# Wave 0's loads in another order: pairs of heads two at a time first, single pairs last, with fewer filling products

## The chip, the cores and the metric

The kernel runs on one core of a Trainium2 chip. Its time is the device time of one execution in microseconds; where a kernel was run several times, the median is given. The engines are named as in the profile: PE (TensorE), PEld (its weight loads), DVE (VectorE), ACT (ScalarE), POOL (GpSimd), SP (SyncE, which here issues nearly all transfers). A transfer moves data between HBM and the on-chip memory (SBUF) and is carried out by 16 DMA engines.

## The reference

Two stages. The first is a decaying linear attention over q, k, v of shape (4 batches, 8 heads, 768 positions, 64), in blocks of positions; `lam` is the decay of each head. The second is a feed-forward layer with a quick gelu on the attention's output, 3072 tokens of 512 features, 2048 hidden ones.

```python
for b in range(nb):                      # blocks of 64 positions
    intra = np.einsum('bhic,bhjc->bhij', qb, kb) * Dmask[None]
    intra = np.einsum('bhij,bhjd->bhid', intra, vb)
    inter = np.einsum('bhid,bhde->bhie', qb * lam_pow[None], kv_state)
    out[:, :, sl] = intra + inter
    kv_state = lam_block[None, :, None, None] * kv_state \
        + np.einsum('bhsd,bhse->bhde', kb * rev_pow[None], vb)
...
h = x @ w_in
g = h * (1.0 / (1.0 + np.exp(-1.702 * h)))
return g @ w_out
```

## The kernel before, in words

The work goes in six waves of 512 tokens. A wave first does its attention, which leaves `xT` (features by tokens, one part per pair of heads), then the first product with w_in (`mlp1`, L511) with the gelu on ACT (L517), then the second product with w_out (`mlp2`, L539). Attention of a later wave is spread among the feed-forward products of the wave before it. Wave 0 has nothing to hide behind: at the start the chip has no data, and everything has to be loaded.

Waves 0 and 1 are special. They take 256 positions of two batches each, so that wave 0 covers batches 0 and 1, and their unit of work is one batch and one pair of heads: (bl, p), bl 0 or 1, p 0 to 3. `UNITS` (L167 to L171) is the order of wave 0's eight units, and the same loop queues their loads: for each entry (bl, p, n) one transfer each for k, q and v, holding n pairs of heads, 128 KB per pair (`load_units`, L86). All are issued by SP except the very first q, which ACT issues (L89).

All loads land in a ring of 50 half slots of 128 KB (`ring`, L83). The function `pump` (L128) hands out places in the order in which the loads were queued: wave 0's q, k, v, then 16 pieces of w_in (256 KB each), seven of the eight halves of w_out (512 KB each), then the loads of wave 1 with the eighth half of w_out among them, then wave 2. A load of more than one half slot starts at an even place. A place is taken again when the load before it there has been read.

For each unit the steps are, in the order of the loop L575 to L610: cast k times its decay (`u_cast_kq` with i=0, on DVE, L280) and q (i=1, on POOL, L280), both one unit ahead; cast v (POOL, L288); turn both by four transposing products (`u_turn`, PE, L298) and copy them from PSUM (L306 on ACT, L308 on DVE); in the next round the scores (L320), the state's product kv (L345), the masking (DVE, L325) and the state's copy (L353 on ACT, L355 on DVE); in the round after that the two output products (L385, L394) and the copy to `xT` (ACT, L398). Before each `u_turn` stands `fill(FILL[i])` (L592): that many 128-column fp32 products of zeros (L271), four to an instruction, which the profile shows as two matmuls for each instruction. `fill(FILL0)` (L568) does 12 of them at the very start. They compute nothing that is used.

Weights are cast to bf16 from the ring piece by piece (`cast_w`, L157): rows 0 to 2 of w_in on POOL (L585, L590), behind the last units' casts in its queue, the others on DVE as they come (L611). Three slices of the first product are begun early: contraction part kc needs the pair kc of both batches and row kc of w_in (L597, L609, L615). The second product of wave 0 runs over the four quarters of w_out in turn (L702), so that it uses w_out as it arrives.

Every engine works through its own queue in order, except that PE takes weight loads ahead.

Of the kernel before, what the change touches and what calls it, by code (L numbers as in the profile page):

```python
# [24 lines left out]
def kernel(  # L25
# [60 lines left out]
    def load_units(w, nm, bl, p, n=2):  # L86

        def go(x):
            eng = nc.scalar if (w, nm, bl, p) == (0, "q", 0, 0) else nc.sync  # L89
            eng.dma_start(  # L90
                out=x.rearrange("s (h c) -> s h c", h=2 * n),
                in_=SRC[nm][2 * w + bl, 2 * p : 2 * (p + n), 0 : 2 * P, :].rearrange("h (q j) d -> q h (j d)", j=2))
            for i in range(n):
                loaded[w, nm, bl, p + i] = x.rearrange("s (n h j d) -> s n h j d", n=n, h=2, j=2)[:, i]
        coming.append((n, [(w, nm, bl, p + i) for i in range(n)], 1, go))
# [69 lines left out]

    A_UNITS, B_UNITS = [(0, p) for p in range(NP)], [(1, p) for p in range(NP)]
    UNITS = []  # L167
    for bl, p, n in [(0, 0, 1), (0, 1, 2), (1, 0, 2), (1, 2, 2), (0, 3, 1)]:
        UNITS += [(bl, p + i) for i in range(n)]
        for nm in "kqv":  # L170
            load_units(0, nm, bl, p, n)  # L171
# [388 lines left out]
                nc.scalar.copy(o, t)  # L560
            store(w, g, o, c)

    FILL0, FILL = 12, (0, 4, 3, 2, 1, 0, 0, 0)
    NF = 3
    KV_ENG = {i: nc.vector if i in (2, 4, 6) else nc.scalar for i in range(1, 9)}

    with tc.manual_schedule():
# [161 lines left out]
        for w in range(2, NW):  # L729
# [5 lines left out]
            n = 4 if w == 2 else 0  # L735
# [48 lines left out]
```

## Time and profile before

| | |
|---|---|
| time, median of 4 runs | 213.84 us (213.06, 213.34, 214.34, 215.96) |
| profiled execution: its own time, and its span | 215.96 us, 214.3 us |
| busy: PE, DVE, ACT, POOL | 205.9, 104.1, 90.0, 34.2 us |
| filling products (L271) | 14 matmuls, 8.8 us |
| first half slots landed (k, q, v of unit 0) | 4.6, 5.3, 5.0 us |
| last load of wave 0 landed | 14.7 us |
| last half of w_out landed | 41.06 us |

All times inside the execution count from the start of the span. A line of a timeline gives the start, the time taken, the engine, the line of the kernel, the operation, out<-in, and how many instructions are merged; in square brackets stands how long the engine had been idle and what ended that. A line of the chain of waits gives start, time and what was being done or waited for. The time of a transfer to landing counts from the start of its issue.

### The profile page before, as it was taken

Reading aid. Unit: us, or ns where it says so; the run is one execution under the profiler, and the core shown is the slowest. Engines: PE = TensorE matmul, PEld = TensorE weight load, DVE = VectorE, ACT = ScalarE, POOL = GpSimd, SP = SyncE. Lnnn points to the kernel's source line nnn. Section 1 sums busy time; section 2 is a strip of 40 time slices with the busy share of each in tenths; the row PEclk is TensorE's granted clock in tenths of the full one; section 3 lists DMA queues with packets and bytes.
Section 4 is the critical chain, followed back from the end, with each engine's and each line's share of the span. In section 5 each row is a group of like instructions: output and inputs, shape, how many; then the busy total and the mean of one; then the engine's idle time right before and its main releaser. Section 6 shows DMA issues by size and latency. Waiting matters only on the chain.

```text
span 214.3 us, 4410 instructions
## 1 busy us (share of the span) xinstructions
PE 205.9 (96%) x1735; PEld 108.6 (51%) x1758; DVE 104.1 (49%) x233; ACT 90.0 (42%) x182; POOL 34.2 (16%) x64
## 2 busy tenths in 40 slices
PE   7999999799999999998999999999999999999994
PEld 3564444357855875443554445554444444444443
DVE  5786635465678775264762445652445232100121
ACT  3776761156633762084511266420276420476000
POOL 6782000362004000004000080000080000000000
PEclk9999999999999999999999999999999999999999
DMA  5999899997999999999999989479990223100112
GB/s 135 300 331 378 279 392 381 293 283 164 224 229 206 139 243 164 235 259 208 185 234 188 264 170 218 93 162 213 227 177 18 52 75 103 71 0 0 49 52 98
DMA packets 95461, 40.15 MB, mean 187 GB/s; under 512 B 76880, under 2 KB 89424, under 8 KB 95440
## 3 DMA queue, kind: packets, MB, share of 16 engines
q1 hardware_dynamic: 95024, 39.73, 79.0%
q8 instruction: 14, 0.23, 0.4%
q10 hardware_dynamic: 416, 0.14, 0.2%
q14 instruction: 7, 0.06, 0.1%
HBM read 27.27 MB, written 6.29 MB: 157 GB/s over the span
## 4 chain that ended last, share of the span: by engine, by line
PE 71%; DMA 19%; SPq 4%; DVE 3%; issue 2%; ACT 0%; DVEq 0%
PE ps_out L539 30%; PE ps_h L511 28%; DMA ring<-in_moe_w_out_dram 8%; DMA ring<-in_moe_w_in_dram 5%; PE ps_s L449 3%; PE ps_o L486 3%; SPq L90 2%; DMA kq<-kqs 2%; DMA ring<-in_k_dram 2%; PE ps_out L554 2%; DMA xT<-xs 2%; PE ps_kv L464 1%; PE ps_o L479 1%; DVE sm L325 1%; PE ps_t L298 1%
## 5 line engine op out<-in xcount | busy, mean ns | idle before, releaser
L511 PE MATMUL ps_h<-xT,w_in 128*128 128x512 bf16 (+1 forms) x439 | 86.0, 348 | 1.1 <-DMA xT<-xs 0.5
L539 PE MATMUL ps_out<-w_out,g_sb 128*128 128x512 bf16 x354 | 81.0, 379 | 2.0 <-DVE w_out L157 1.1
L517 ACT ACTIVATE g_sb<-ps_h 128x512 bf16<-128x512 f32 (+1 forms) x112 | 58.5, 538 | 57.5 <-PE ps_h L511 56.2
L511 PEld LDWEIGHTS <-w_in 128*128 128x128 bf16 x448 | 42.9, 98 | 38.5 <-issue 0.8
L539 PEld LDWEIGHTS <-g_sb 128*128 128x128 bf16 x368 | 35.0, 98 | 41.1 <-issue 1.6
L546 DVE COPY o_sb<-ps_out 128x512 f32<-128x512 f32 x17 | 11.8, 691 | 51.0 <-PE ps_out L539 49.8
L456 DVE SCALAR_TENSOR_TENSOR sm<-ps_s,inv_pow,mask 128x512 bf16<-128x512 f32 x32 | 22.6, 747 | 24.6 <-PE ps_s L449 24.4
L489 ACT CAST xs<-ps_o 128x512 bf16<-128x512 f32 x16 | 9.4, 585 | 24.1 <-PE ps_o L486 24.1
L438 POOL CAST v_bd<-ring 128x512 bf16<-128x512 f32 x8 | 6.8, 885 | 56.7 <-PE ps_h L511 56.7
L438 POOL CAST v_sb<-ring 128x512 bf16<-128x512 f32 x8 | 6.9, 906 | 37.7 <-PE ps_h L511 23.5
L280 POOL TENSOR_TENSOR kqs<-ring,kq_pow 128x256 bf16<-128x256 f32 x14 | 8.5, 625 | 26.2 <-DMA ring<-in_q_dram 24.4
L325 DVE TENSOR_TENSOR sm<-ps_s,mask 128x512 bf16<-128x512 f32 x16 | 10.6, 685 | 3.1 <-PE ps_s L320 3.0
L436 DVE TENSOR_SCALAR kqs<-ring,q_pow 128x256 bf16<-128x256 f32 x32 | 9.8, 348 | 4.0 <-DMA ring<-in_q_dram 4.0
L468 DVE SCALAR_TENSOR_TENSOR kv<-kv,blk,ps_kv 64x256 bf16<-64x256 bf16 x24 | 11.4, 476 | 0.2
L436 DVE TENSOR_SCALAR kqs<-ring,k_pow 128x256 bf16<-128x256 f32 x32 | 10.5, 370 | 0.2
L271 PE MATMUL ps_f<-zeros 128*128 128x512 f32 (+3 forms) x14 | 8.8, 748 | 1.1 <-DVE zeros L187 1.1
L280 DVE TENSOR_TENSOR kqs<-ring,kq_pow 128x256 bf16<-128x256 f32 x18 | 8.6, 503 | 1.7 <-ACT kq_pow L218 1.3
L157 DVE CAST w_out<-ring 128x512 bf16<-128x512 f32 x16 | 6.1, 424 | 6.5 <-DMA ring<-in_moe_w_out_dram 6.5
L544 ACT COPY o_sb<-ps_out 128x512 f32<-128x512 f32 x6 | 3.5, 586 | 13.2 <-PE ps_out L539 12.6
L157 DVE CAST w_in<-ring 128x512 bf16<-128x512 f32 x13 | 5.5, 427 | 4.8 <-DMA ring<-in_moe_w_in_dram 4.8
L288 POOL CAST v_bd<-ring 128x256 bf16<-128x256 f32 x16 | 7.0, 459 | 2.9 <-DMA ring<-in_v_dram 2.9
L449 PE MATMUL ps_s<-kq 64*128 64x128 bf16 x128 | 6.4, 219 | 1.1 <-DMA kq<-kqs 0.8
(71 smaller groups left out, 115.8 us busy)
## 6 DMA issues: line engine op xcount, KB each, us to landing
ring<-in_k_dram SPq DMA_DIRECT2D x23, 256.0 KB, 4.6
ring<-in_q_dram SPq DMA_DIRECT2D x23, 256.0 KB, 4.8
ring<-in_v_dram SPq DMA_DIRECT2D x23, 256.0 KB, 4.8
out_dram<-o_sb SPq DMA_DIRECT2D x23, 256.0 KB, 2.5
ring<-in_moe_w_in_dram SPq DMA_DIRECT2D x16, 256.0 KB, 6.3
ring<-in_moe_w_out_dram SPq DMA_DIRECT2D x8, 512.0 KB, 9.5
ring<-in_k_dram SPq DMA_DIRECT2D x2, 128.0 KB, 4.4
ring<-in_v_dram SPq DMA_DIRECT2D x2, 128.0 KB, 4.1
```

Source lines behind the costliest of these rows:

```text
L157: eng.tensor_copy((w_in_sb if kind == "in" else w_out_sb)[j][:, r, :], read(kind, j, r))
L280: eng.tensor_tensor(kqs_of[w, p][:, bl, i].rearrange("s j h d -> s h j d"), read(w, "kq"[i], bl, p), tab, op=MUL)
L325: nc.vector.tensor_tensor(sm.rearrange("s h j t -> s h (j t)"), s_ps.pop((w, bl, p))[:, :, 0 : 2 * P], mask2.to_broadcast([P, 2, 2 * P]), ...
L436: nc.vector.tensor_scalar(kqs[:, i, :, h, :], x[:, :, p, h, :], scalar1=(k_pow, q_pow)[i][:, 2 * p + h : 2 * p + h + 1], scalar2=None, op0 ...
L438: nc.gpsimd.tensor_copy(v_sb[w % 2][:, p], read(w, "v")[:, :, p])
L449: nc.tensor.matmul(s[:, h, b, :], t[hd(h), 0, b, :], t[hd(h), 1, b, :], start=True, stop=True)
L456: nc.vector.scalar_tensor_tensor(sm[:, h], s[:, h], inv_pow[:, 2 * p + h : 2 * p + h + 1], mask.to_broadcast([P, B, P]), op0=MUL, op1=MUL)
L468: nc.vector.scalar_tensor_tensor(new[hd(h), p], old[hd(h), p], blk2[hd(h), p : p + 1], t[hd(h), :, hd(h)], op0=MUL, op1=ADD)
L511: nc.tensor.matmul(t[:, bs[0] * P : bs[1] * P], w_in_sb[fc // CW][:, kc, :].rearrange("s (R m c) -> s R c m", R=2, c=2)[:, fc % CW // 2, f ...
L517: nc.scalar.activation(g_tile(w)[:, fc, c], h_ps.pop((w, fc))[:, c], GELU)
L539: nc.tensor.matmul(t, g_of[w][:, fc, g * P : (g + 1) * P], w_out_sb[j][:, fc % CW, :], start=(fc == 0), stop=(fc == FFC - 1))
L546: nc.vector.tensor_copy(o, t)
```

## The change

The order of wave 0's loads, and with it that of its units, becomes: pairs 0 and 1 of batch 0, pairs 0 and 1 of batch 1, pairs 2 and 3 of batch 0, then pair 2 of batch 1 and pair 3 of batch 1 as transfers of one pair each. Before, it was pair 0 of batch 0 alone, pairs 1 and 2 of batch 0, pairs 0 and 1 of batch 1, pairs 2 and 3 of batch 1, and pair 3 of batch 0 alone. There are fifteen transfers both times. The number of filling products before the turns of units 1 to 4 goes from 4, 3, 2, 1 to 2, 1, 1, 0; the twelve at the very start stay.

```diff
     A_UNITS, B_UNITS = [(0, p) for p in range(NP)], [(1, p) for p in range(NP)]
     UNITS = []
-    for bl, p, n in [(0, 0, 1), (0, 1, 2), (1, 0, 2), (1, 2, 2), (0, 3, 1)]:
+    for bl, p, n in [(0, 0, 2), (1, 0, 2), (0, 2, 2), (1, 2, 1), (1, 3, 1)]:
         UNITS += [(bl, p + i) for i in range(n)]
         for nm in "kqv":
             load_units(0, nm, bl, p, n)
...
-    FILL0, FILL = 12, (0, 4, 3, 2, 1, 0, 0, 0)
+    FILL0, FILL = 12, (0, 2, 1, 1, 0, 0, 0, 0)
     NF = 3
```

## The prediction

> **What bounds the kernel now.** I read the page first, for the shares over the whole span, then the chain that ended last in order of time, then the timelines of PE, DVE and POOL over the first 46 us, which is where the change acts.
>
> The page, engine shares and the DMA and clock rows:
>
> ```profile
> PE 205.9 (96%) x1735; PEld 108.6 (51%) x1758; DVE 104.1 (49%) x233; ACT 90.0 (42%) x182; POOL 34.2 (16%) x64
> PEclk9999999999999999999999999999999999999999
> DMA  5999899997999999999999989479990223100112
> ```
>
> PE is busy nearly throughout, so it is easy to call the kernel PE-bound everywhere. But in the first eight slices (about 43 us) the DMA engines are full as well. Which of the two ends last there is told by the chain of waits:
>
> ```profile
> 11.69 6.49 DMA ring<-in_moe_w_in_dram
> 18.18 0.02 issue
> 18.20 5.29 DMA ring<-in_moe_w_in_dram
> 23.48 0.02 issue
> 23.50 0.44 DVE w_in L157
> 23.94 0.02 SPq L123
> 23.96 0.03 issue
> 23.99 17.07 DMA ring<-in_moe_w_out_dram x2
> 41.06 0.02 issue
> 41.08 0.44 DVE w_out L157
> 41.52 0.04 issue
> 41.56 1.58 PE ps_out L539 x6
> ```
>
> Until 41.1 us the chain is one stream of loads on SP's queue (q, k, v of wave 0, then w_in, then w_out), not arithmetic. PE joins it only at the last half of w_out. PE's timeline and DVE's, at the same place:
>
> ```profile
> 19.56 12.69 PE L511 MATMUL ps_h<-xT,w_in 128*128 128x512 bf16 x57
> 32.09 8.37 PE L539 MATMUL ps_out<-w_out,g_sb 128*128 128x512 bf16 x37
> 41.56 1.58 PE L539 MATMUL ps_out<-w_out,g_sb 128*128 128x512 bf16 x6 [1.11 <-DVE w_out L157]
> ```
> ```profile
> 28.78 0.43 DVE L157 CAST w_in<-ring 128x512 bf16<-128x512 f32 x1 [2.26 <-DMA ring<-in_moe_w_in_dram]
> 41.08 0.76 DVE L157 CAST w_out<-ring 128x512 bf16<-128x512 f32 x2 [2.38 <-DMA ring<-in_moe_w_out_dram]
> ```
>
> From 19.56 PE runs without a gap until 32.09 + 8.37 = 40.46, then stands 1.11 us for the last half of w_out. That is the number to carry: whatever wave 0's attention gains, PE only waits longer here, and whatever it loses, up to 1.11 us, is paid out of this wait. Only the landing at 41.06 counts. There is little to be gained on the way either: the last row of w_in is cast by 29.21, and feed-forward slice 12, whose gelu starts at 29.70 and whose last product takes about 0.21, needs it at about 29.4.
>
> **The change part by part.**
>
> *Order of loads.* Fifteen transfers before, fifteen after, 3 MB both times, on the same queues (the first q on ACT, the rest on SP); three singles move from the front to the end. An issue lasts 0.45 us for 128 KB and 0.46 to 0.51 for 256 KB among the first ones, so SP's time for the issues is the same. From issue starts and times to landing of before, the k, q, v of the five groups land at 4.6, 5.3, 5.0; 6.2, 7.1, 8.0; 8.9, 9.8, 10.7; 11.5, 12.5, 13.4; 13.8, 14.3, 14.7 us: about 0.90 us per 256 KB and 0.45 per 128 KB. Landing is thus a matter of bytes queued ahead. Put on the same line by bytes, the new groups land (estimates): first pair k about 5.3, q 5.9, v 6.65; pairs (0,1) of batch 1 at 7.55, 8.4, 9.3; pairs (2,3) of batch 0 at 10.2, 11.1, 12.0; the singles at 12.5, 12.9, 13.4 and 13.8, 14.3, 14.7. The last byte comes at 14.7 as before, so w_in follows when it did: stream 0.
>
> Two places could move the stream. (a) The start: in eight slices of 0.3125 us from 1.9 to 4.4 us the DMA engines move 122, 121, 107, 146, 176, 177, 209 and 264 GB/s against a steady 293. The missing 1022 x 0.3125 = 319 KB are 1.1 us of stream. If bigger first transfers filled all of it, that is -1.1. I take 0, since by 2.5 us 640 KB are issued and only some 75 KB moved, so it is not the issues that the engines lack. (b) The end: SP's issue number n waits for the landing of number n-8 (w_in row 10 is issued at 18.20, row 2 landed at 18.18). With six singles among the eight, w_in's row 0 waits for the q of pairs (2,3), 11.1 instead of 10.70; row 1 12.0 instead of 11.21; row 2 12.5 instead of 11.69; row 3 12.9 instead of 12.49; row 4 at 13.4 as before. The 0.8 of row 1 is the upper end. I take 0: at 12.0 wave 0 still has 2.7 us of landings queued, and a first packet follows its issue by 1.1 us (0.80, first bytes at 1.9).
>
> Transfers of 128 KB are what a rule of the Trainium skill speaks against: "DMA: Bandwidth & Descriptors", section "Anatomy of one DMA", gives each transfer about 2.0 us of fixed cost besides its bytes. If the three more singles at the end paid it one after another, that would be an estimate by the page of 6 us, or 219.8. In this trace the three singles at the end land 0.45 us apart, at the rate of the large ones, with seven others in flight; by that row it is 0, and 213.8.
>
> *Ring.* One empty half slot that single and double loads left at each end is saved, so everything behind moves by two half slots of 50. Followed by hand, each later load takes the place of the same earlier load as before up to wave 3's q, where the wrap differs (the places of units read some 15 us earlier): 0. No transpose or store stands on SP's queue in wave 0.
>
> *Order of units.* Pairs (0,1) of batch 1 come third and fourth. POOL is the strict queue here, as it casts q and v in turn:
>
> ```profile
> 9.86 1.18 POOL L280 TENSOR_TENSOR kqs<-ring,kq_pow 128x256 bf16<-128x256 f32 x2 [0.65 <-DMA ring<-in_q_dram]
> 10.99 0.94 POOL L288 CAST v_bd<-ring 128x256 bf16<-128x256 f32 x2
> 12.55 1.18 POOL L280 TENSOR_TENSOR kqs<-ring,kq_pow 128x256 bf16<-128x256 f32 x2 [0.62 <-DMA ring<-in_q_dram]
> 13.68 0.94 POOL L288 CAST v_bd<-ring 128x256 bf16<-128x256 f32 x2
> 14.58 0.61 POOL L280 TENSOR_TENSOR kqs<-ring,kq_pow 128x256 bf16<-128x256 f32 x1
> 15.40 0.61 POOL L157 CAST w_in<-ring 128x512 bf16<-128x512 f32 x1 [0.21 <-DMA ring<-in_moe_w_in_dram]
> ```
>
> It waits for q, and the PE's turn of a unit starts when q is cast. With 0.61 a q and 0.46 a v, in the order of the code, the new q casts end at 6.5 (the power table of ACT is what unit 0 waits for, as before), 7.7, 9.1 (q landing at 8.4, the new wait), 10.6, 11.7, 13.2, 13.9 and 15.4. Behind the new wait on POOL stands the v of unit 1 (8.47 before, 9.1 after), which PE's kv product of that unit waits for. Before, the last q cast ended at 14.58 + 0.61 = 15.19. Then POOL takes w_in's row 0 at 15.40 both times. DVE's third k cast waits until 7.55 and ends at 8.2, in time for the copy behind it at 8.27. Sum: 0.2 us later at the last q cast, hidden: PE's turn of the last unit was at 15.74.
>
> *Filling products.* Ten 128-column fp32 products become four. The four groups took 1.19, 0.92, 0.70 and 0.49 us; they become 0.70, 0.49, 0.49 and none: 3.30 - 1.68 = 1.6 us of PE's time between 6.8 and 12.4. Nearly none reaches the end: the new turns start at about 7.85, 9.1, 10.6, 11.8, 13.3, 14.5 and 15.7, against 7.85, 9.26, 10.86, 12.24, 13.30, 14.55 and 15.74, since the casts pace them, and from 13.30 on there was no filling before. If the attention gained 0.2 or lost 0.2, the 1.11 us wait takes it up.
>
> Sum: stream 0, attention 0 to 0.2 hidden by 1.11, everything after 41.56 the same program. The profiled execution took 215.96 with a span of 214.3, the slowest of four; the median is 213.84, and to that I add 0: **213.8**. The likeliest case's own range, from (b) and a part of (a): 213.1 to 214.6.
>
> **The rivals.**
>
> *The stream starts fuller* (a): for it, the 319 KB missing; against it, the 640 KB issued in time. The landing at 41.06 comes up to 1.1 earlier, PE's wait of 1.11 is just used up: 212.7. More is not to be had, as PE itself has no gap from 19.56 on.
>
> *The singles starve the stream* (b): for it, row 1 issued 0.8 later; against it, the queue. 213.84 + 0.8 = 214.6.
>
> *The clock falls* (slower). The filling products are there to keep PE at work. The page's clock row says 9 throughout, but the durations don't: the first filling products follow each other at 0.85 us, the ones at 6.82 take 1.19 for two with their ends; turn 0 takes 0.63 and the later ones 0.38. So PE ran at half speed for its first 6 us of work, whatever that row says. If thinner work between 8 and 13 us sends it back, five units lose at least 0.63 - 0.38 = 0.25 each, 1.25 together, and the dense products after 17 us run 6 us at half speed again, 3.0 lost: 4.25 late at 40.46. From 1.11 on it decides: 213.84 + 4.25 - 1.11 = 217.0. Against it: the new gaps between units are 0.4 to 0.5 us each by my times, and the units without filling from 13.30 to 17 kept the 0.4 us turns.
>
> A rule bears on this one: "TensorE: Matmul & The Clock Gate", section "Why this matters for your kernels", puts the limit at idle gaps of some 3 us. By it the clock stays and the sum is 213.8; no row here shows where the limit lies.
>
> **How the numbers follow.** As predicted 0.70; fuller start 0.12; starved 0.08; clock 0.10. The predicted time is the likeliest's. The range must leave out no more than 2 in 10: I leave out the clock case and take in 212.7 and 214.6, the first with 0.1 and the second with 0.6 added for scatter (the four runs lie at 213.06 to 215.96, with the long tail upwards): 212.6 to 215.2. One per cent, 2.1 us, is about what a measurement of this kernel can tell from no change. Only the clock case is over it: slower 0.10. A gain of 2.1 is out of reach of every case, as 1.11 is all the wait there is; 0.02 for what I have overlooked. Same 0.88.
>
> **What would show it.** Right: PE's wait before the last half of w_out at 0.9 to 1.4 us, its landing at 41.1 within 0.8; first k landing near 5.3, q of batch 1's first pairs near 8.4 with POOL waiting on it; row 0 of w_in cast at 15.4; dense products from about 19.5. Wrong: that landing more than 1 us off (the stream moved); turns of 0.6 us after 8 us or dense products 0.43 apart (the clock); or PE no longer waiting at w_out (attention late by more than 1.11).

## The result, and the profile after

The changed kernel takes 218.11 us in the median of 43 runs (213.51 to 221.44), the kernel before 214.14 in 64 (212.92 to 216.27). The granted clock is the share of TensorE's full clock that the profile records. By its mean the 43 runs fall into two groups: 24 lie between 217.95 and 221.44 (median 219.4) with 0.953 to 0.969, and the others between 213.51 and 216.1 with 0.990 to 1.000. The ratio of the two kernels, 1.0039 (1.002 to 1.0057), compares, like every ratio below, only runs close to the fastest of their own kernel, so here it holds none of the 24; the medians hold all. The change therefore does two things: it costs some 0.8 us in the better group, and in over half of the runs the clock falls for long, which costs some 4.6 us more. Of the better group, eight runs (0.990 to 0.992) had a short fall and eleven none; the median of those eleven, 214.7, is 0.6 us above that of before. The profiled execution is one of the 24: 219.03 us, span 217.3.

The same page rows as before:

```profile
PE 208.9 (96%) x1733; PEld 110.3 (51%) x1756; DVE 101.7 (47%) x233; ACT 90.7 (42%) x182; POOL 34.3 (16%) x64
PEclk9955899999999999999999999999999999999999
DMA  4999999999993699999999989577982222200112
```

PE's share is 96% again, though it did no more useful work: part of its busy time was at half clock. The row to look at is the second, where the third to fifth slices (11 to 27 us) are low. Stretches cut at the changes of the clock (columns: start and end, length, PE, PEld, DVE, ACT and POOL busy with instruction counts, granted clock, DMA share, GB/s):

```profile
6.75:10.15 3.40, 1.49 (x18) 0.90 (x20) 1.20 (x4) 2.42 (x7) 1.81 (x4) 1.00 1.12 291
10.16:13.57 3.41, 3.41 (x43) 2.46 (x41) 2.64 (x6) 1.40 (x3) 2.88 (x6) 0.50 1.11 289
...
20.40:23.80 3.40, 3.07 (x39) 1.52 (x38) 0.82 (x3) 1.77 (x4) 0.00 (x0) 0.50 1.01 374
23.82:27.00 3.18, 3.18 (x33) 1.50 (x30) 3.18 (x9) 1.90 (x5) 0.00 (x0) 1.00 1.01 291
```

The clock is full for 3.41 us, of which PE works 1.49; then it is half for 13.65 us, four times 3.41, although PE is shown as busy in nearly all of it; and full again once the dense products run. Half of 13.65 over a span of 217.3 is 0.031, the 0.969 of this run. The other mean clocks are the same sum for one (0.99), two (0.984), five (0.961) and six (0.953) such stretches of 3.41 us. Where a run below is said to have lost a stretch, it ran one at half clock. Before, the first full stretch had PE busy throughout:

```profile
7.05:10.45 3.40, 3.40 (x46) 1.92 (x47) 2.86 (x6) 2.21 (x5) 2.64 (x6) 1.00 1.18 293
```

What PE did around it, and the chain of waits (start, time, what):

```profile
1.12 5.49 PE L271 MATMUL ps_f<-zeros 128*128 128x512 f32 x6 [1.12 <-DVE zeros L187]
6.86 0.29 PE L298 MATMUL ps_t<-ident,kqs 128*128 128x128 bf16 x2 [0.25 <-DVE kqs L280]
8.92 0.29 PE L298 MATMUL ps_t<-ident,kqs 128*128 128x128 bf16 x2 [1.78 <-POOL kqs L280]
...
25.31 12.69 PE L511 MATMUL ps_h<-xT,w_in 128*128 128x512 bf16 x57
37.84 8.37 PE L539 MATMUL ps_out<-w_out,g_sb 128*128 128x512 bf16 x37
```
```profile
1.29 6.82 DMA ring<-in_q_dram
8.26 0.62 POOL kqs L280
8.92 0.29 PE ps_t L298 x2
```

PE turns k of unit 0 at 6.86, then stands 1.78 us until q is cast; q of the first two pairs, issued at 1.29, landed at 8.11. From 10.16 on the units run at half clock: without filling before them they take 1.69 us each (turns at 15.15, 16.84, 18.53) instead of 1.2. The dense products begin at 25.31 instead of 19.56, and no wait for w_out is left in front of the second product. 5.75 late less the 1.11 us of that wait is 4.64. Against the median of before this execution is 4.9 us longer. The two spans differ by only 3.0, as the profiled execution of before, the slowest of its four, loses time later that this one does not: between 80 and 100 us its PE is busy for 18.64 us, here for 19.84.

### The profile page after: what moved, and what is told of

The parts are those of the page before. It is cut to its first block, busy times and chain, and to the rows that moved or that the text cites. A ratio compares the mean times of both kernels' runs of the same rounds, so it can differ in the third digit from the quotient of the medians.

```text
span 217.3 us, 4403 instructions
## 1 busy us (share of the span) xinstructions
PE 208.9 (96%) x1733; PEld 110.3 (51%) x1756; DVE 101.7 (47%) x233; ACT 90.7 (42%) x182; POOL 34.3 (16%) x64
## 4 chain that ended last, share of the span: by engine, by line
PE 89%; DMA 7%; issue 1%; ACT 1%; POOL 0%; DVE 0%; SPq 0%; POOLq 0%
PE ps_h L511 36%; PE ps_out L539 35%; DMA ring<-in_q_dram 3%; PE ps_t L298 3%; PE ps_s L449 3%; PE ps_o L486 3%; DMA kq<-kqs 2%; PE ps_s L320 2%; DMA out_dram<-o_sb 2%; PE ps_o L394 2%; PE ps_out L554 2%; PE ps_kv L464 1%; PE ps_o L479 1%; PE ps_o L385 1%; PE ps_f L271 1%
## 5 line engine op out<-in xcount | busy, mean ns | idle before, releaser
L438 POOL CAST v_sb<-ring 128x512 bf16<-128x512 f32 x8 | 6.4, 838 | 37.7 <-DMA ring<-in_v_dram 37.7
L436 DVE TENSOR_SCALAR kqs<-ring,k_pow 128x256 bf16<-128x256 f32 x32 | 9.8, 350 | 0.2
L298 PE MATMUL ps_t<-ident,kqs 128*128 128x128 bf16 x64 | 7.4, 254 | 2.1 <-POOL kqs L280 1.8
L271 PE MATMUL ps_f<-zeros 128*128 128x512 f32 (+2 forms) x12 | 7.7, 779 | 1.1 <-DVE zeros L187 1.1
L280 DVE TENSOR_TENSOR kqs<-ring,kq_pow 128x256 bf16<-128x256 f32 x18 | 7.6, 453 | 2.3 <-ACT kq_pow L218 2.3
L308 DVE COPY kq<-ps_t 128x512 bf16<-128x512 bf16 x8 | 3.2, 422 | 10.9 <-PE ps_t L298 10.8
L298 PEld LDWEIGHTS <-kqs 128*128 128x128 bf16 x64 | 5.1, 113 | 5.5 <-POOL kqs L280 2.1
```

The source lines that it names most:

```text
L271: nc.tensor.matmul(t[:, 0 : c * P], zeros, zeros[:, 0:1].to_broadcast([P, c * P]), start=True, stop=True)
L280: eng.tensor_tensor(kqs_of[w, p][:, bl, i].rearrange("s j h d -> s h j d"), read(w, "kq"[i], bl, p), tab, op=MUL)
L298: nc.tensor.transpose(t_ps[w, bl, p][:, i, j, :], kqs_of[w, p][:, bl, i, j].rearrange("s h d -> s (h d)"), ident)
L436: nc.vector.tensor_scalar(kqs[:, i, :, h, :], x[:, :, p, h, :], scalar1=(k_pow, q_pow)[i][:, 2 * p + h : 2 * p + h + 1], scalar2=None, op0 ...
L438: nc.gpsimd.tensor_copy(v_sb[w % 2][:, p], read(w, "v")[:, :, p])
```

## The experiments

Theory A, at first: the larger first transfers bring the first q late, PE stands idle, and the clock falls for that. Theory B: the thinner filling between the units lets it fall. C: it belongs to the chip. Later A2: both are needed, idle time to lower the clock and thin filling to keep it low. The runs below were on three chips, called I to III; none of those on chip I is of the changed kernel itself.

| run | chip | median us (before) | ratio, interval | runs with a mean clock of 0.976 or less | of 0.98 to 0.992 | all runs |
|---|---|---|---|---|---|---|
| e1_fill_only | I | 213.98 (214.22) | 0.9985 (0.9947 to 1.0022) | 0 | 0 | 10 |
| e2_order_only | I | 215.24 | 1.0062 (1.0028 to 1.0096) | 0 | 2 | 7 |
| e3_fill0_20 | I | 214.99 | 1.0038 (1.0017 to 1.0059) | 0 | 0 | 10 |
| e4_q_on_sp | I | 214.36 | 1.0019 (0.9983 to 1.0055) | 0 | 0 | 10 |
| e5_changed_again | II | 219.26 (214.31) | none | 3 | 0 | 4 |
| e6_first_pair_thin | II | 216.59 | 1.0099 (1.0065 to 1.0134) | 0 | 6 | 10 |
| e7_fill4_first | II | 215.55 | 1.0035 (0.9991 to 1.0079) | 2 | 3 | 10 |
| e8_no_fill | II | 217.24 | 1.0154 (1.008 to 1.0229) | 4 | 0 | 4 |
| e9_changed_control | II | 215.79 (213.65) | 1.0022 (0.9981 to 1.0063) | 4 | 2 | 10 |
| e10_single_first | II | 214.94 | 1.0021 (0.9975 to 1.0066) | 3 | 0 | 10 |
| e11_fill0_20_again | II | 214.96 | 1.0029 (0.9988 to 1.007) | 0 | 1 | 10 |
| e12_fill_later | II | 215.73 | 1.0031 (0.9987 to 1.0074) | 2 | 4 | 10 |
| e13_control | III | 218.08 (213.54) | none | 3 | 0 | 4 |
| e14_fill_only | III | 213.71 | 1.0002 (0.9973 to 1.0031) | 0 | 0 | 10 |
| e15_order_only | III | 216.57 | 1.0161 (1.0117 to 1.0204) | 0 | 4 | 4 |
| e16_q_on_sp | III | 213.8 | 1.0013 (0.9986 to 1.0041) | 0 | 0 | 10 |

Of 96 runs of the kernel before beside these, none had a clock under 0.998.

**The changed kernel as control** (e5, e9, e13), unedited.

> The changed kernel itself, on the same chip as the next three. Theory A2 (PE's idle time before unit 0's q turn lowers the clock, and the thinner filling after it does not bring it back until the dense products): clock 0.95 to 0.97 in about half of the runs, those 217.5 to 221.5 us, the rest 213.5 to 216. Theory C (the fall belongs to one chip or one day): no run below 0.98.

> The changed kernel once more, as the control on the chip of the next three: the earlier kernels that kept the clock had run on another chip than the ones that lost it. Theory A2 (idle time of PE in a window lowers the clock, thin filling keeps it low): clock at or below 0.97 in about half of the runs. Theory C (it is the chip): the next three behave as this one does.

> The changed kernel as the control for the next three, which had run on a chip without it. If this chip shows the fall: clock at or below 0.97 in 3 to 7 of 10 runs.

The clock fell to 0.97 or less in 10 of 18 runs, on both chips where it was tried; so C falls, and where a kernel kept the clock on the chip of a control, that is due to its edit.

**Filling alone** (e1, e14): the kernel before with the changed filling.

```diff
-    FILL0, FILL = 12, (0, 4, 3, 2, 1, 0, 0, 0)
+    FILL0, FILL = 12, (0, 2, 1, 1, 0, 0, 0, 0)
```

> The kernel before with the changed kernel's filling products alone (2, 1, 1, 0). Theory A (the changed first transfers bring q late, PE stands idle some 1.8 us around unit 0's turn, and the clock falls for that): nothing falls, granted clock 1.00 in all runs, 213 to 215 us, ratio 0.997 to 1.004. Theory B (too little filling between the units lets the clock fall): granted clock 0.95 to 0.97 in a good part of the runs, and these at 218 to 221 us.

> The loads and units of before with the changed filling (2, 1, 1, 0), beside the control. Theory A2 (idle time from the late first q has to come first): clock at or above 0.99 in all runs, ratio 0.996 to 1.002. If thin filling alone is enough at these numbers: at or below 0.98 in some runs, as without any filling.

No fall in 20 runs and no difference in time: B as it stood falls. PE in e14, where it waits for w_out as before, though only 0.22 us (1.00 in e1's profile):

```profile
40.35 1.57 PE L539 MATMUL ps_out<-w_out,g_sb 128*128 128x512 bf16 x6 [0.22 <-DVE w_out L157]
```

**No filling at all** (e8), on the loads of before: `FILL` all 0.

> The kernel before without any filling between units (0 everywhere); its first loads come early, so PE has no long idle time. Theory A2: clock 0.99 to 1.00 in all runs, time 213 to 215. Theory B (thin work alone lets the clock fall): clock below 0.98 in a good part of the runs, and those at 217 or more.

The expectation of A2 was missed: the clock fell in all four runs. PE was idle 0.85 us before unit 1's last turn and busy 1.90 of the 3.39 us ahead of the fall:

```profile
5.85:9.24 3.39, 1.90 (x25) 1.02 (x24) 2.24 (x6) 2.68 (x7) 2.53 (x6) 1.00 1.16 297
9.26:22.89 13.63, 13.62 (x174) 7.27 (x173) 9.45 (x20) 7.68 (x17) 6.94 (x13) 0.50 1.10 355
```

So the idle time of 1 to 2 us that the changed order brings is not needed: without any filling the clock falls too. B was right in this form, and wrong only for the numbers of the change.

**Order alone** (e2, e15): the changed loads and units with the filling of before.

> The changed kernel with the filling of before (4, 3, 2, 1). Theory A: first q lands at about 8 us again, PE's idle time before unit 0's q turn is again 1.5 to 2 us, clock below 0.98 in about half of the runs, those at 217.5 to 221 us. Theory B: clock 1.00 in all runs; time then 214.5 to 215, as the load stream still comes some 0.8 late.

> The changed loads and units with the filling of before (4, 3, 2, 1), beside the control. Theory A2: the idle time is there, the filling brings the clock back within a window or two: some runs at 0.98 to 0.992, none or one at or below 0.97, median 215 to 216.5. If the idle time alone decides: at or below 0.97 as often as in the control.

The idle time is there (0.80 and 1.40 us in e15), the clock falls, but the filling brings it back after one or two stretches:

```profile
5.24:8.63 3.39, 1.19 (x7) 0.27 (x5) 0.76 (x2) 3.19 (x12) 0.82 (x2) 1.00 1.15 309
8.65:12.05 3.40, 3.40 (x21) 1.75 (x20) 1.84 (x5) 0.88 (x3) 2.56 (x6) 0.50 1.15 289
12.07:20.00 7.93, 7.76 (x148) 5.13 (x146) 6.45 (x15) 5.83 (x13) 6.37 (x12) 1.00 0.94 295
```

A alone expected a far fall (0.976 or lower) in half of the runs and got none in eleven; for the numbers of this change A2 stands: the far fall needs both halves. But the order alone is not free. Its median is 1.0 us above that of before on chip I and 3.0 us on chip III, where the control is 4.5 us above; in e15 all four runs lost one or two stretches.

**Which filling brings it back** (e7: 4, 1, 1, 0; e12: 2, 3, 2, 1).

> The changed kernel with only the filling before unit 1's turn put back to 4 (4, 1, 1, 0). If the work right behind the idle time decides, within the same window of some 3.4 us: no run below 0.98, about 215 us. If the thin stretch that follows decides: clock 0.95 to 0.97 in a good part of the runs, as in the changed kernel.

> The changed kernel with the filling before units 2, 3 and 4 put back to 3, 2, 1 and that before unit 1 left at 2. The idle time is as in the control, so the clock may still fall; if the later filling brings it back after one or two windows of 3.4 us, the clock is at or above 0.98 in all runs and the time at most 217. If the fall lasts until the dense products whatever stands between the units: 0.96 to 0.97 and 218 or more in about half of the runs.

Neither decides: each still has 2 of 10 runs at 0.961 or less, besides those with one or two stretches (3 and 4). Neither part of the filling settles it alone, and neither of the two pictures in either expectation came clean; whether each helps a little cannot be told from ten runs.

**Covering the idle time** (e3, e11): the changed kernel with more products at the very start.

```diff
-    FILL0, FILL = 12, (0, 2, 1, 1, 0, 0, 0, 0)
+    FILL0, FILL = 20, (0, 2, 1, 1, 0, 0, 0, 0)
```

> The changed kernel with 20 instead of 12 filling products at the very start, which at half clock reach to about 10 us instead of 6.6 and cover PE's idle time. Theory A: clock 1.00 in all runs, 214.5 to 215.5 us: the late stream stays, the clock does not fall. Theory B: clock still falls in about half of the runs, as the thin stretch between the units after it is the same: median about 218.

> The changed kernel with 20 filling products at the very start, on the control's chip. Theory A2: PE has no idle time before 8.5 us, clock at or above 0.99 in all runs, 214.5 to 215.8. Theory C: clock at or below 0.97 as often as in the control.

One run in 20 lost a single stretch, none fell far, with the same thin filling afterwards. PE goes over from the products to unit 0 without a gap:

```profile
4.69 3.94 PE L271 MATMUL ps_f<-zeros 128*128 128x512 f32 x6
8.46 0.38 PE L298 MATMUL ps_t<-ident,kqs 128*128 128x128 bf16 x4
```

The 0.8 us of the late start stays: unit 0 begins at 8.46, the dense products at 21.0.

**Why the first q is late** (e4, e16): SP issues it too.

```diff
-            eng = nc.scalar if (w, nm, bl, p) == (0, "q", 0, 0) else nc.sync
+            eng = nc.sync
```

> The changed kernel with the first q issued by SP like all others, not by ACT. If q is late because the DMA engines share themselves between two queues, of which SP's holds k, v and the next pairs: q lands at 6.3 to 6.8, v at 7.2 to 7.6, PE's idle time shrinks to 0.3 to 0.5 us, and the clock stays in nearly all runs (214.5 to 215). If q is late because the first 512 KB take that long wherever they are queued: q still lands at 7.5 or later and the clock falls in about half of the runs.

> The changed kernel with the first q on SP's queue, beside the control. Theory A2 with the two queues as the reason for the late q: q lands at 6.2 to 6.5, PE idle time under 0.4 us at a time, clock at or above 0.99 in all runs, 213.8 to 214.8. If it was the chip: at or below 0.97 in some runs.

The first transfers of the changed kernel, then of e16 (time from issue to landing last):

```profile
ring<-in_k_dram SPq DMA_DIRECT2D x1, 256.0 KB, 4.8
ring<-in_q_dram ACTq DMA_DIRECT2D x1, 256.0 KB, 6.8
ring<-in_v_dram SPq DMA_DIRECT2D x1, 256.0 KB, 6.6
lam_p<-in_lam_dram ACTq DMA_DIRECT2D x1, 4.0 KB, 4.5
```
```profile
ring<-in_k_dram SPq DMA_DIRECT2D x1, 256.0 KB, 4.7
ring<-in_q_dram SPq DMA_DIRECT2D x1, 256.0 KB, 5.1
ring<-in_v_dram SPq DMA_DIRECT2D x1, 256.0 KB, 5.4
```

On SP's queue q lands second, 5.1 us after its issue; on ACT's it lands last, after 6.8, and v too lands later after its issue (6.6 against 5.4). On ACT's queue it landed at 6.67 to 8.11 us in the ten profiles with the whole changed order, on SP's at 6.28 and 6.37. After the products at the start PE's longest idle time ahead of the dense products was 0.31 us in e4's profile and 0.52 in e16's (0.3 to 0.5 and under 0.4 were expected). With q on SP no run in 20 lost a stretch, and the time is that of before within the interval. The step is shown: the place of one transfer on a second queue is what the 4 us hang on.

Why that place is late is only in part clear. ACT issues the 4 KB of `lam` ahead of q, on the same queue. In the changed kernel's profile that queue moved 63 packets but less than 5 KB from 2.5 to 3.5 us, and 0.02 MB from 3.5 to 4.5, while SP's moved 0.08 and 0.15; only from 4.5 to 6.5 did it move 0.22 beside SP's 0.39. So q's bytes hardly began to move before 3.5 us. Whether q would be in time on ACT's queue without `lam` ahead of it was not tried.

**Size of the first transfers against the order of the units** (e6: the order of units as before, first transfers of two pairs, filling of before; e10: the changed order, first transfers single).

```diff
-    for bl, p, n in [(0, 0, 1), (0, 1, 2), (1, 0, 2), (1, 2, 2), (0, 3, 1)]:
+    for bl, p, n in [(0, 0, 2), (0, 2, 1), (1, 0, 2), (1, 2, 2), (0, 3, 1)]:    # e6
...
-    for bl, p, n in [(0, 0, 2), (1, 0, 2), (0, 2, 2), (1, 2, 1), (1, 3, 1)]:
+    for bl, p, n in [(0, 0, 1), (0, 1, 1), (1, 0, 2), (0, 2, 2), (1, 2, 1), (1, 3, 1)]:    # e10
```

> The kernel before in which the first two groups are swapped in size (pairs 0 and 1 of batch 0 as one transfer, pair 2 alone), so that the units keep the order of before and only the first transfers are larger; filling as before (4, 3, 2, 1). Theory A2: first q lands at 7 to 8 us, dense products start 1.3 to 1.9 us later than before, time 214.7 to 215.5, clock at or above 0.99. If the order of the units is what costs: first q still late, but dense products start within 0.5 us of before, 213.8 to 214.3.

> The changed kernel whose first group is split into two transfers of one pair for each of k, q and v (18 transfers; units in the changed order, filling 2, 1, 1, 0). Theory A2: first q lands at 5.2 to 5.6 us, PE idle under 0.5 us before unit 0's last turn, clock 0.99 to 1.00 in all runs, 213.5 to 215 us. If the order of the units or the thin filling lowers the clock: at or below 0.97 in some runs, as in the control.

e6: q landed at 7.52, six of ten runs lost one stretch, and the time is further up than expected, 2.3 us above before. The size of the first transfers by itself makes q late and the clock fall for a stretch; the order of the units is not needed for that. e10 missed its expectation: the first q landed at 5.04 and the early idle time was gone, but in its profile the q of batch 1's first pairs landed at 9.27, 1.97 us behind k, and PE stood 1.39 us within unit 2's turn. The clock stayed in that execution, but three of ten runs fell. That late q is a second weak place of the order; that it is what made those three fall is not shown.

## Why the prediction was wrong

**The step that failed** is "Put on the same line by bytes, the new groups land (estimates): first pair k about 5.3, q 5.9, v 6.65". Bytes queued ahead give the landing on one queue: with q on SP's they came at 5.5, 6.4 and 7.3, then 8.2, 9.1, 10.0 (e16; estimates 7.55, 8.4, 9.3), 0.2 to 0.7 late. Across two queues they do not. Here q landed at 8.11, 2.2 us behind its estimate, and v at 7.92. Before, q's 128 KB on ACT's queue had already landed after the v issued behind it (5.31 against 5.06; so too in e1, and the other way round in e8 and e14). That row spoke against the estimate, and the prediction used it without drawing this from it. The Trainium skill, "DMA: Bandwidth & Descriptors", section "Queues, rings and completion order", says that a DMA engine takes turns between the queues that have work for it. These landings agree with it in kind: with q on ACT's queue both queues moved bytes at the same time, as told above, so q shared the engines with v and with the next pairs' k. With q on SP's queue, where it landed at 6.37, the time is 213.8, as predicted (e16; 214.36 in e4, where before has 214.22).

**From there**: the wait on POOL came at unit 0 (4.0 us for q in the profile); at unit 2, where the prediction had it, the profile shows none of 0.2 us or more, and one of 0.53 us at unit 4. PE's longest gap was 1.0 to 1.8 us in the profiles with these first transfers, q on ACT's queue and 12 products at the start. It lay in front of or within unit 0's turn, where the prediction had none; it had gaps of "0.4 to 0.5 us each by my times" between units.

**The clock rival** was the right mechanism, at 0.10 and 217.0; it happened in over half of the runs, at 219.4. I let it off for those small gaps. Its price was mis-sized: it had 0.25 us for each of five units and 3.0 us for dense products at half clock, 4.25 late. In the profile the units after the fall take some 0.5 us more each, nearly all of the 13.65 us at half clock is theirs, and the dense products are 5.75 late, of which 1.7 stand already at unit 1's turn (9.54 against 7.85); in other runs the mean clock tells of up to six stretches, 20 us. The Trainium skill's limit of some 3 us of idle time, weighed there ("TensorE: Matmul & The Clock Gate", section "Why this matters for your kernels"), is contradicted by these runs: in two profiles the longest idle times before the fall were 1.78 and 1.10 us, and without filling 0.85. But idle time alone does not decide either: in profiles of e2, e5 and e12 idle times of 1.51, 1.29 and 1.09 us were not followed by a fall. The window of 3413 ns that the same page gives in "What's actually happening" agrees with 3.41 and 13.65.

**The stream** was nearly right. Wave 0's last load landed at 15.1 to 15.8 us in the profiles of the changed order but two (14.7 before), the last half of w_out at 40.0 to 42.0, and the profiles with the loads of before have that at 38.9 to 41.1: no shift that the scatter shows. The singles at the end did not starve it; they landed 0.36 to 0.48 us apart, but for the last one in those two profiles, the changed kernel's (17.07) and e10's (16.62), 1.8 and 2.0 us behind. The 2.0 us a transfer that the prediction weighed (the Trainium skill, "DMA: Bandwidth & Descriptors", section "Anatomy of one DMA") are fitted there to transfers issued by GpSimd; these are issued by SP, and in the other profiles no such cost shows between them.

**The 1.11 us wait** as a cushion was right in kind: e16's dense products start at 19.93 and the time is that of before. As a number it was one execution's: 1.11, 1.00 and 0.22 in three profiles with the loads of before and some filling. In all profiles of the changed order it is used up, and a start at 20.0 to 21.4 where the clock stayed shows as the 0.8 us.

**The filling** by itself costs and brings nothing, as predicted (1.0002, 0.9973 to 1.0031); the wrong part was to cost it without the idle time beside which it stands. **The ring** moved without effect: e16 has the same ring and the same time as before.

**The range** (212.6 to 215.2) left the clock case out at 0.10, and that is where the median lies.

What stays open: how much work in a window keeps the clock. In 16 profiles with recorded changes, PE's busy time in the first full window was 1.19 to 2.21 us in the six where the clock then fell, and 2.21 to 3.40 in nine of the ten where it stayed. That nearly sorts them, but in e5's, with 1.60, it stayed as well, and during the half clock PE was busy for 3.40 of 3.41 us without bringing it back. So the busy time of the records alone does not decide; what does was not found.

## What to carry to other kernels

Before thinning out the work that only keeps PE going, look at what it stands beside: less filling cost nothing by itself and a later first operand 1 to 3 us, and together they cost some 5 us in over half of the runs. Do not work out landings by bytes across two queues: here a transfer on a second queue took 6.8 us instead of 5.1, behind a small one of its own queue and beside all that was on the first. And where a stage is made of small products, price a fall of the clock until the next dense stage (three to six windows of 3.41 us in the far falls here), not for one window, and compare several runs' mean clock before trusting one time.

## What the runs showed that I had not expected

- With the thinner filling the small products of a unit mostly do not bring the clock back although PE counts as busy: four windows at half clock with PE at 3.07 to 3.41 of 3.4 us. At half clock the same work fills more of the time: a unit's turn takes 0.61 us instead of 0.4.
- Where the windows lie differs from run to run: in the profiles with clock changes recorded, the full clock begins at 4.11 to 7.15 us, always in steps of 3.41 afterwards. The same kernel both keeps and loses the clock. That the place of the idle time in the window decides would fit e10's profile, where 1.39 us of idle time lie across a boundary at 9.71 and the clock stays, and that of e5, where 1.25 us lie across one at 7.52. But in e12's profile 1.09 us lie within a window and the clock stays too. It was not tried by itself.
- The granted clock reads 1.00 before the first recorded change, while the products there take the time of half clock: in e3 the filling products start 0.85 us apart before it and 0.43 after.
- The 4 KB of `lam` landed at 3.97 to 4.52 us with 128 KB behind them on ACT's queue in five profiles, and at 4.61 to 5.50 with 256 KB behind them; with q on SP it was 4.52 once and 5.13 once, so the cause is not settled.
